# A two-layer chain of MLPs behind attention: the last 768 tokens of the first MLP as a 2x2 block product of seven multiplications

## The chip, the cores and the metric

The kernel runs on one core of one Trainium2 chip. The metric is the device time of one execution in microseconds, and the median of the runs is compared. A profile is one execution, recorded by the hardware. PE is the matrix engine, DVE the vector engine, ACT the scalar engine, POOL the GpSimd engine, SP the queue that issues nearly all transfers. Names such as `h<-xt,w` mean: this instruction writes tile `h` and reads tiles `xt` and `w`.

## The reference

Causal windowed attention over 4 sequences of 576 tokens (8 heads of 64, window 64) gives x of 2304 tokens by 512. Two MLPs follow; nothing is masked or routed:

```python
x = attention(q, k, v)                      # 2304 x 512
h = x @ moe_w_in                            # 512 -> 2048
x = softplus(h) @ moe_w_out                 # 2048 -> 512
gate = sigmoid(x @ moe2_w_gate)             # 512 -> 1536
out = (gate * (x @ moe2_w_val)) @ moe2_w_out    # 1536 -> 512
```

The weights come in a wide format as pairs of 32-bit words. The kernel makes of each value a part "hi" and a rest "lo", and each product is three matmuls: hi*hi, hi*lo, lo*hi (`mm3`).

## The kernel before

**Attention.** 36 groups of 64 query tokens (all heads at once): scores on PE, maximum and exponential on DVE and ACT, the sum's reciprocal, the scaling on POOL, a transposition, and the product with the values on PE (`att_scores` to `att_values`). The first 8 groups run ahead of the first MLP. The transposition is on PE for the groups of the first two token blocks (`att_transpose`); for the others DVE transposes 32x32 pieces and two transfers through DRAM finish it (`att_blocks`, `att_send`, `att_fetch`). `att_hi` and `att_lo` write the result as hi and lo into the block's tile `xt`.

**First MLP.** The tokens stand in five blocks, `BLOCKS1 = [512, 384, 384, 512, 512]`. For each block and each of 16 slices f of 128 hidden features, `m1_proj` makes h (4 chunks of the 512 inputs, 12 matmuls, each as wide as the block), ACT takes softplus (`m1_act`) and splits off hi (`g_hi`), DVE makes lo (`g_lo`), and `m1_out` adds the slice's share to four accumulators (12 matmuls). PE runs `m1_out` two projections behind `m1_proj`; h has two PSUM banks, so the projection after next waits for `g_lo`. A finished block is copied out of PSUM and sent to DRAM (`m1_copy`, `m1_send`, tensor `x2d`).

**Weights of the first MLP** are split once, during the first block: `w_scale` on ACT, `w_shift`, `w_sign`, `w_low` on DVE, `w_hi` on ACT, `w_lo` on DVE, one pair of slices (w1 of f, w2 of f-2) for each projection.

**Second MLP.** It already uses the scheme of seven products: 768 tokens at a time (two halves of 384, `HALF`), the inputs' two halves, and gate and value as the two column blocks. For each of 12 slices, seven sums of weight blocks were made while the first MLP ran (`c_sums`, `c_sum4`, split in `c_hi`, `c_lo`, stored to DRAM with `c_send` as `wcd`) and come back as `wc` (`wc_load`, 1792 KB, two buffers). Seven sums of token blocks are made per 768 tokens (`x2_load`, `x2_sum`, `x2_hi`, `x2_lo`). PE makes seven products of 6 matmuls with 384 columns (`m2_prod`), DVE recombines them (`m2_after`, helper `tt`), and `m2_out` adds to six accumulators of 128 tokens each, with 18 matmuls of 512 columns.

**What sets the order.** The PE order is written out (`slots`). Everything else ahead of the second MLP is placed on its engine by a planner in the kernel (`lead_in`): it walks through the work with due times from `events`, costs from `traits` and a few weights in the constants, and emits one fixed order for each engine. Each engine then works in that order, so an instruction that waits holds back all behind it on its engine. SP issues transfers in its own fixed order.

## Time and profile before

| what | us |
|---|---|
| median of three runs | 895.02 (894.74 to 895.33) |
| the profiled execution | 895.09 |
| its span, first to last instruction | 893.3 |
| PE busy in the span | 885.0 |
| DVE, ACT, POOL busy | 523.8, 400.0, 153.8 |
| granted TensorE clock | 1.00 of full speed nearly throughout (mean 0.999) |

Three stretches follow each other: the lead-in to 31 us, in which attention for the first 512 tokens runs and weights arrive; the first MLP with the rest of attention, from 31 us to 471 us; the second MLP, from 471 us to the end. A matmul's record is longer than its share of the stream, since one starts before the last has ended; what one costs is read from start to start.

### The profile page before, as it was taken

To read this page: it belongs to the slowest core of one execution; us is meant where nothing else is said; L and a number is where in the kernel's file an instruction comes from. 1 tells how busy PE (TensorE), PEld (TensorE's weight loads), DVE (VectorE), ACT (ScalarE), POOL (GpSimd) and SP (SyncE) were. 2 spreads that over 40 slices of the span, in tenths; PEclk is the share of its full clock that TensorE was granted. 3 is DMA by queue.
4 is the path that set the end of the run, shared out by engine and by line. 5 is a ranking of instruction groups with operands and counts; after the bars stand their busy time and mean duration, and the time that the engine had idled before them with its cause. 6 is when DMAs were issued, how large, how long until landed. Compare 5 with 4: busy or idle time off the path is not lost.

```text
span 893.3 us, 13510 instructions
## 1 busy us (share of the span) xinstructions
PE 885.0 (99%) x5035; PEld 797.6 (89%) x5035; DVE 523.8 (59%) x921; ACT 400.0 (45%) x892; POOL 153.8 (17%) x157
## 2 busy tenths in 40 slices
PE   9999999999999999999999999999999999999997
PEld 7788789999999888888889999999999999999996
DVE  4898876556555756455515667668445447444444
ACT  6867857546764755345323333334222125222222
POOL 4001102102110220002001333331111112111110
PEclk9999999999999999999999999999999999999999
DMA  9946346766885764683307565545454445544441
GB/s 349 397 151 210 134 163 210 246 199 226 270 268 205 243 234 165 209 287 130 130 1 256 220 254 203 208 174 216 179 209 159 159 164 209 183 165 165 165 165 72
DMA packets 56210, 177.58 MB, mean 199 GB/s; under 512 B 6096, under 2 KB 21456, under 8 KB 51536
## 3 DMA queue, kind: packets, MB, share of 16 engines
q1 hardware_dynamic: 56000, 176.58, 56.0%
q8 instruction: 40, 0.66, 0.3%
q14 instruction: 26, 0.21, 0.1%
q10 hardware_dynamic: 144, 0.13, 0.0%
HBM read 139.72 MB, written 36.96 MB: 198 GB/s over the span
## 4 chain that ended last, share of the span: by engine, by line
PE 97%; DVE 1%; ACT 1%; POOL 0%; issue 0%; POOLq 0%
PE h L394 17%; PE h L396 17%; PE h L395 17%; PE acc L394 11%; PE acc L395 11%; PE acc L396 11%; PE at L289 3%; PE at L376 2%; PE at L396 2%; PE at L395 2%; PE at L394 2%; PE acc L289 1%; PE h L406 1%; PE acc L338 0%; POOL w L330 0%; PE at L338 0%
## 5 line engine op out<-in xcount | busy, mean ns | idle before, releaser
L512 DVE TENSOR_TENSOR w<-h,w 128x384 f32<-128x384 f32 x216 | 117.0, 556 | 159.7 <-PE h L396 157.0
L394 PE MATMUL h<-w,wc 128*128 128x384 f32 x504 | 169.0, 335 | 0.1
L396 PE MATMUL h<-w,wc 128*128 128x384 f32 x504 | 169.0, 335 | 0.0
L395 PE MATMUL h<-w,wc 128*128 128x384 f32 x504 | 168.8, 335 | 0.0
L524 POOL TENSOR_TENSOR g<-w,g 128x384 fp32r<-128x384 f32 x70 | 74.0, 1057 | 296.7 <-ACT g L517 252.1
L394 PE MATMUL acc<-g,w 128*128 128x512 f32 (+1 forms) x320 | 119.5, 374 | 0.0
L394 PE MATMUL h<-xt,w 128*128 128x512 f32 (+1 forms) x320 | 119.4, 373 | 0.1
L396 PE MATMUL h<-xt,w 128*128 128x512 f32 (+1 forms) x320 | 117.9, 368 | 1.0 <-DVE w L187 1.0
L396 PE MATMUL acc<-g,w 128*128 128x512 f32 (+1 forms) x320 | 117.7, 368 | 0.0
L395 PE MATMUL acc<-g,w 128*128 128x512 f32 (+1 forms) x320 | 117.6, 368 | 0.0
L395 PE MATMUL h<-xt,w 128*128 128x512 f32 (+1 forms) x320 | 117.6, 368 | 0.0
L436 DVE TENSOR_TENSOR g<-h,g 128x512 fp32r<-128x512 f32 (+1 forms) x80 | 50.7, 634 | 84.1 <-ACT g L430 83.8
L394 PEld LDWEIGHTS h<-w,wc 128*128 128x128 f32 x504 | 94.6, 188 | 2.4 <-DVE w L512 0.4
L395 PEld LDWEIGHTS h<-w,wc 128*128 128x128 f32 x504 | 94.6, 188 | 2.0
L396 PEld LDWEIGHTS h<-w,wc 128*128 128x128 f32 x504 | 94.6, 188 | 0.0
L423 ACT ACTIVATE h<-h 128x512 f32<-128x512 f32 (+1 forms) x80 | 43.2, 540 | 108.7 <-PE h L396 108.3
L517 ACT CAST g<-w 128x384 fp32r<-128x384 f32 x72 | 36.9, 513 | 117.5 <-DVE w L512 117.5
L396 PEld LDWEIGHTS h<-xt,w 128*128 128x128 f32 x320 | 60.1, 188 | 9.2 <-DVE w L187 1.7
L394 PEld LDWEIGHTS h<-xt,w 128*128 128x128 f32 x320 | 60.1, 188 | 8.4 <-issue 0.6
L394 PEld LDWEIGHTS acc<-g,w 128*128 128x128 f32 x320 | 60.1, 188 | 8.0
L396 PEld LDWEIGHTS acc<-g,w 128*128 128x128 f32 x320 | 60.1, 188 | 7.6
L330 POOL TENSOR_TENSOR p<-p,st 128x512 f32<-128x512 f32 (+1 forms) x28 | 27.8, 996 | 226.2 <-DVE st L325 165.2
(129 smaller groups left out, 1440.9 us busy)
## 6 DMA issues: line engine op xcount, KB each, us to landing
wc<-wcd SPq DMA_DIRECT2D x36, 1792.0 KB, 7.3
qk<-in_qk SPq DMA_DIRECT2D x28, 512.0 KB, 5.1
wcd<-raw SPq DMA_DIRECT2D x24, 512.0 KB, 3.5
w<-in_w SPq DMA_DIRECT2D x16, 512.0 KB, 9.6
raw<-in_w SPq DMA_DIRECT2D x16, 512.0 KB, 4.6
v<-in_vt SPq DMA_DIRECT2D x25, 256.0 KB, 3.8
raw<-in_wg SPq DMA_DIRECT2D x12, 512.0 KB, 4.6
raw<-in_wv SPq DMA_DIRECT2D x12, 512.0 KB, 6.1
```

The lines of the kernel that those rows point to most:

```text
L289: nc.tensor.matmul(out=s[:, j, :w], lhsT=t[:, 0, j, :], rhs=t[:, 1, j, :w], start=g >= NG0, stop=g >= NG0 or j == NPAIR - 1)
L330: nc.gpsimd.tensor_tensor(out=p[:, :, :w], in0=p[:, :, :w], in1=st[:, 2, :].unsqueeze(2).to_broadcast([P, NPAIR, w]), op=ALU.mult)
L376: nc.tensor.matmul(out=o[h * Q:(h + 1) * Q, j, :], lhsT=v[:w, (2 * j + h) * Q:(2 * j + h + 1) * Q], rhs=pt[:w, h, j], start=True, stop=True)
L394: nc.tensor.matmul(out=o, lhsT=lh, rhs=rh, start=first, stop=False)
L395: nc.tensor.matmul(out=o, lhsT=lh, rhs=rl, start=False, stop=False)
L396: nc.tensor.matmul(out=o, lhsT=ll, rhs=rh, start=False, stop=last)
L406: nc.tensor.matmul(out=idle["out"], lhsT=t[:, 0, :P], rhs=t[:, 1], start=True, stop=True)
L423: nc.scalar.activation(out=t, in_=t, func=AF.Softplus)
L436: nc.vector.tensor_tensor(out=g[:, 1, :n], in0=t, in1=g[:, 0, :n].bitcast(F32), op=ALU.subtract)
L512: nc.vector.tensor_tensor(out=out, in0=a, in1=b, op=op)
L517: nc.scalar.copy(out=g[:, 0, :HALF], in_=t)
L524: eng.tensor_tensor(out=g[:, 1, :HALF], in0=t, in1=g[:, 0, :HALF].bitcast(F32), op=ALU.subtract)
```

## The change

The first MLP now runs 1536 tokens in three blocks of 512 as before, and the last 768 tokens by the scheme of seven products.

- `SPLIT = 4`: the second block's first four slices are done for each half of 256 tokens apart (`UNITS`), so that their first half needs four groups of attention instead of eight. These matmuls have 256 columns.
- The last 768 tokens' attention goes to DRAM as floats (`att_out`, `att_put`, tensor `x1d`) and comes back in quarters (`x2_load`).
- For each pair of w1 slices (8 "quads", `NQ1`), DVE adds hi and lo again (`c_join`), and the sums are made and stored like those of the second MLP. There are 20 sets `wcd` instead of 12, and 44 loads `wc` instead of 36.
- A quad: seven products (`s_prod`, 42 matmuls of 384 columns), a copy on ACT (`s_copy`), seven recombinations on DVE (`s_mix`), four softplus on ACT (`s_act`), four splits (`s_hi` on ACT, `s_lo` on DVE or POOL). `s_out` adds to six accumulators of 128 tokens with w2 as the moving operand: 12 outputs of 3 matmuls of 512 columns, in runs of three.
- The accumulators hold tokens in rows, while the second MLP reads features in rows. So each is transposed in 32x32 pieces by DVE on the way out (`s_drain`) and stored by four transfers (`s_send`) of 64 KB each, in pieces of 128 bytes.
- The planner has other numbers: attention, joins and sums are placed by times (`DENSE`, `NEXT`, `REST`, `COMBO1`, `COMBO2`), eight instead of six groups run in the first block's time, and a transfer behind the lead-in is allowed 0.8 instead of 1.5 us of margin (3.8 us for `x2_load`).

PE's matmuls by count, from the two programs: first MLP, 512 columns 1152 before and 1056 after; 384 columns 768 and 0; 256 columns 0 and 192; in the quads 336 of 384 and 288 of 512 columns. Transpositions of later groups on PE: 24 and 32. Scores, values, the lead-in's matmuls and the second MLP's are as many as before.

```diff
-BLOCKS1 = [512, 384, 384, 512, 512]
+BLOCKS1, NS1, SPLIT = [512, 512, 512], 1, 4
-SLACK, NEAR = 0.15, .3
+SLACK, NEAR = 0.15, 0.4
+DENSE, NEXT, REST = (6.9, 11.0, 9.6), (62.8, 97.8), (120.5, 273.9)
+COMBO1, COMBO2, WOF, WOG, XT = (144.2, 12.9), (237.5, 17.3), 9.0, 13.0, 33.91
+URGE, FAR_MARGIN, X_MARGIN, HURRY = 40, 0.8, 3.0, 1.5
...
+    def c_join(q, k):
...
+        nc.vector.tensor_tensor(out=c_bits(q)[:, k], in0=w[:, 0], in1=w[:, 1], op=ALU.add)
...
+        if b == 1 and SPLIT:
+            UNITS += [(b, 0, n // 2, 0, SPLIT), (b, n // 2, n, 0, SPLIT), (b, 0, n, SPLIT, NF1)]
...
+    def att_put(g):
+        t0 = g * Q - NT1
+        nc.sync.dma_start(out=x1d[:, :, t0:t0 + Q].rearrange("k p n -> p k n"), in_=x_t.pop(g))
...
+    def s_prod(s, f, k):
+        o = h_t[s, f, k] = psum(f"h{(7 * (s * NQ1 + f) + k) % 2}")[:, :HALF]
+        product(o, s, f, k)
+
+    def s_copy(s, f):
+        nc.scalar.copy(out=half(0, 0), in_=h_t.pop((s, f, 0)))
+
+    def s_mix(s, f, k):
+        m1, u2, lo, hi, sa = (half(0, i) for i in range(5))
+        o = h_t.pop((s, f, k))
+        if k == 1:
+            tt(u2, o, m1, ALU.add)
+        elif k == 2:
+            tt(sa, o, m1, ALU.add)
+        elif k == 3:
+            tt(lo, o, u2, ALU.add)
+        elif k == 4:
+            tt(hi, o, lo, ALU.add)
+            tt(u2, o, u2, ALU.add)
+        elif k == 5:
+            tt(lo, lo, o, ALU.subtract)
+        else:
+            tt(sa, o, u2, ALU.add)
...
+    def s_out(s, f, j, c):
+        g, w = g_t[s, f, j], w_t["w2", 2 * f + j % 3 % 2 + (j == 2)]
+        cols = slice(c * P % HALF, c * P % HALF + P)
+        mm3(token_acc(s, c), g[:, 0, cols], g[:, 1, cols], w[:, 0, :], w[:, 1, :], f == 0 and j < 2,
+            f == NQ1 - 1 and j > 1)
+
+    def s_drain(s, c):
+        x = x_t[s, "y", c] = main.tile([P, 512], F32, tag="stage", name="x2", bufs=STB)
+        nc.vector.transpose(out=x, in_=acc_t[s, c])
+
+    def s_send(s, c):
+        x, t0 = x_t.pop((s, "y", c)), NT1 + 2 * s * HALF + c * P
+        o = x2d[:, :, t0:t0 + P].rearrange("c (b x) n -> x (c b) n", x=32)
+        for a in range(4):
+            nc.sync.dma_start(out=o[:, :, 32 * a:32 * (a + 1)],
+                              in_=x[32 * a:32 * (a + 1)].rearrange("x (k t) -> x k t", t=32))
...
+        late_q = [(s_out, s, f, j, 3 * j + i) for j in range(2) for i in range(3)]
+        outs = tail
+        for entry in "M0 M1 o0 o1 o2 M2 M3 o3 o4 o5 M4 M5 a0 a1 a2 M6 a3 a4 a5".split():
...
+        tail = [(s_out, s, f, j, (0, 3)[j - 2] + i) for j in (2, 3) for i in range(3)]
...
-                done[key] = dma + 0.85 + MARGIN
+                done[key] = dma + 0.85 + (MARGIN if start < OPEN else FAR_MARGIN + X_MARGIN * (key[0] is x2_load))
```

Where the order moves, in three places. First DVE in the first block, about its projection of f = 11. Before, in the rows from the `g_lo` of f = 10 to that of f = 11 (`g<-h`, line 436; lines 187 and 164 are `w_lo` and `w_shift`, 303 and 306 the maximum of a group):

```order
L436 TENSOR_TENSOR g<-h_956,g 128x512
L187 TENSOR_TENSOR w_1007<-w_860,w_1007 128x512 x2
L187 TENSOR_TENSOR w_1032<-w_860,w_1032 128x512 x2
L164 TENSOR_SCALAR w_1050<-w_1050 128x1024
L303 SCALAR_TENSOR_TENSOR p<-at,mask 128x512
L306 TENSOR_REDUCE st<-p 128x4
L303 SCALAR_TENSOR_TENSOR p<-at,mask 128x512
L306 TENSOR_REDUCE st<-p 128x4
L436 TENSOR_TENSOR g<-h_1035,g 128x512
```

Now, the end of the same stretch (line 483 is `g_lo`, 196 `w_lo`, 177 and 182 `w_sign` and `w_low`, 359, 360 and 424 the end of two groups):

```order
L359 TENSOR_SCALAR st<-st 128x4
L360 RECIPROCAL st<-st 128x4
L424 TENSOR_TENSOR xt<-at,xt 128x4x64 x2
L177 SCALAR_TENSOR_TENSOR w_1081<-raw,w_1081 128x1024
L196 TENSOR_TENSOR w_1156<-w_1081,w_1156 128x512
L182 SCALAR_TENSOR_TENSOR w_1081<-raw,w_1081 128x1024
L483 TENSOR_TENSOR g<-h_1062,g 128x512
L402 COPY pt<-at 128x512
L483 TENSOR_TENSOR g<-h_1134,g 128x512
```

The `g_lo` of f = 11 has moved down past the second half of two groups and two more passes over weights, to two rows ahead of the next one.

Second, DVE beside the work on the last tokens of the first MLP. Before, in the last block (line 489 is `x2_lo`, 164 to 173 the three passes over a pair of weights of the second MLP):

```order
L436 TENSOR_TENSOR g<-h_4099,g 128x512
L489 TENSOR_TENSOR w_4150<-xn_t_3835,w_4150 128x384
L436 TENSOR_TENSOR g<-h_4137,g 128x512
L489 TENSOR_TENSOR w_4185<-xn_t_3836,w_4185 128x384
L164 TENSOR_SCALAR bits<-bits 128x1024
L168 SCALAR_TENSOR_TENSOR bits<-raw,bits 128x1024
L173 SCALAR_TENSOR_TENSOR bits<-raw,bits 128x1024
L436 TENSOR_TENSOR g<-h_4172,g 128x512
```

Now, from the start of the second quad (line 553 is `s_mix`, 595 `s_lo`, 173 to 182 the three passes, 215 to 217 `c_sums`, 247 `c_lo`):

```order
L553 TENSOR_TENSOR w_3650<-h_3807,w_3650 128x384
L173 TENSOR_SCALAR bits<-bits 128x1024
L177 SCALAR_TENSOR_TENSOR bits<-raw,bits 128x1024
L182 SCALAR_TENSOR_TENSOR bits<-raw,bits 128x1024
L553 TENSOR_TENSOR w_3650<-h_3840,w_3650 128x384
L553 TENSOR_TENSOR w_3650<-h_3848,w_3650 128x384
L247 TENSOR_TENSOR raw<-bits,raw 128x512
L595 TENSOR_TENSOR g_3866<-w_3650,g_3866 128x384
L215 TENSOR_TENSOR sums<-bits 128x256
L216 TENSOR_TENSOR sums<-sums,bits 128x256
L217 TENSOR_TENSOR bits<-bits 128x256
L553 TENSOR_TENSOR w_3650<-h_3874,w_3650 128x384 x2
```

Each recombination stands between passes that prepare weights of the second MLP, and the three passes stand ahead of the second and third.

Third, SP at the start of the second MLP. Before (line 461 is `m1_send`, 239 `wc_load`, 135 a load of `wo`):

```order
L239 DMA wc<-wcd_74 128x3584
L461 DMA x2d<-x_4528 128x512
L461 DMA x2d<-x_4531 128x512
L461 DMA x2d<-x_4534 128x512
L461 DMA x2d<-x_4537 128x512
L135 DMA raw<-in_wo 128x1024
L239 DMA wc<-wcd_75 128x3584
```

Now (line 616 is `s_send`, 257 `wc_load`, 144 a load of `wo`):

```order
L257 DMA wc<-wcd_83 128x3584
L616 DMA x2d<-x_4790 32x16x32 x4
L616 DMA x2d<-x_4799 32x16x32 x4
L616 DMA x2d<-x_4825 32x16x32 x4
L144 DMA raw<-in_wo 128x1024
L616 DMA x2d<-x_4857 32x16x32 x4
L616 DMA x2d<-x_4866 32x16x32 x4
L257 DMA wc<-wcd_84 128x3584
L616 DMA x2d<-x_4886 32x16x32 x4
```

Four stores of 256 KB have become 24 of 64 KB, 20 of which stand ahead of the third slice's `wc`.

## Rows read from the trace of the kernel before

**Rows 1.** The page: span, busy time by engine, chain that ended last by engine.

```profile
span 893.3 us, 13510 instructions
PE 885.0 (99%) x5035; PEld 797.6 (89%) x5035; DVE 523.8 (59%) x921; ACT 400.0 (45%) x892; POOL 153.8 (17%) x157
PE 97%; DVE 1%; ACT 1%; POOL 0%; issue 0%; POOLq 0%
```

**Rows 2.** Timeline of PE (start, length, line, names, shape), two projections, four slices apart.

```profile
427.14 0.39 PE L394 MATMUL h<-xt,w 128*128 128x512 f32 x1
...
448.90 0.39 PE L394 MATMUL h<-xt,w 128*128 128x512 f32 x1
```

**Rows 3.** Timeline of PE in the second MLP: outputs of 512 columns, then products.

```profile
600.24 0.39 PE L394 MATMUL acc<-w,g 128*128 128x512 f32 x1
...
601.63 0.33 PE L394 MATMUL h<-w,wc 128*128 128x384 f32 x1
...
602.67 0.33 PE L394 MATMUL h<-w,wc 128*128 128x384 f32 x1
```

**Rows 4.** Timeline of PE: the first product of two slices in succession, second MLP.

```profile
586.72 0.33 PE L394 MATMUL h<-w,wc 128*128 128x384 f32 x1
...
598.16 0.33 PE L394 MATMUL h<-w,wc 128*128 128x384 f32 x1
```

**Rows 5.** Timeline of PE: transpositions of two groups; scores of two groups.

```profile
76.74 1.03 PE L338 MATMUL at<-ident,p 128*128 128x128 f32 x8
...
122.10 1.95 PE L289 MATMUL at<-qk 128*128 128x128 f32 x16
```

**Rows 6.** Timeline of PE: the one idle time inside the first MLP, and its releaser.

```profile
94.46 0.50 PE L396 MATMUL h<-xt,w 128*128 128x512 f32 x1 [0.96 <-DVE w L187]
```

**Rows 7.** Busy time of the engines by stretch (us, and instructions).

```profile
core 0: us, PE busy (x) PEld busy (x) DVE busy (x) ACT busy (x) POOL busy (x), PEclk, DMA share, GB/s
34.00:134.00 100.00, 99.03 (x557) 81.85 (x556) 86.18 (x128) 73.71 (x144) 6.73 (x7) 1.00 0.53 188
134.00:300.00 166.00, 166.00 (x1152) 161.46 (x1151) 99.97 (x190) 100.80 (x248) 23.18 (x22) 1.00 0.69 227
300.00:470.00 170.00, 170.00 (x874) 140.82 (x873) 86.15 (x144) 79.97 (x169) 22.12 (x20) 1.00 0.53 177
```

**Rows 8.** Groups of DVE by line and shape: count, busy us, mean ns.

```profile
L512 DVE TENSOR_TENSOR w<-h,w 128x384 f32<-128x384 f32 x216 | 117.0, 556 | 159.7 <-PE h L396 157.0 <-issue 1.3 <-ACT w L533 1.2
L168 DVE SCALAR_TENSOR_TENSOR bits<-raw,bits 128x1024 uint32<-128x1024 uint32 x14 | 17.8, 1273 | 0.4
L306 DVE TENSOR_REDUCE st<-p 128x4 f32<-128x512 f32 x25 | 17.2, 686 | 0.9
L303 DVE SCALAR_TENSOR_TENSOR p<-at,mask 128x512 f32<-128x512 f32 x25 | 17.1, 684 | 16.0 <-PE at L289 15.8
L389 DVE TENSOR_TENSOR xt<-at,xt 128x256 fp32r<-128x256 f32 x36 | 14.4, 413 | 6.9 <-ACT xt L384 6.6
```

**Rows 9.** Waits: ACT's `w_scale` for the second MLP's weights (total, times, longest).

```profile
ACT bits L160 <- DMA raw<-in_wv: 11.9, 5, 3.8
```

**Rows 10.** Transfers: count, KB each, median us from issue to landing.

```profile
wc<-wcd SPq DMA_DIRECT2D x36, 1792.0 KB, 7.3
pt<-pd SPq DMA_DIRECT2D x84, 64.0 KB, 3.3
x2d<-x SPq DMA_DIRECT2D x12, 256.0 KB, 2.2
```

**Rows 11.** Timeline of PE: the first product of the second MLP.

```profile
470.67 0.33 PE L394 MATMUL h<-w,wc 128*128 128x384 f32 x1
```

More of the change, by code (lines that the diff above doesn't have):

```diff
@@ new lines, in c_hi, with c_lo, c_send @@
+    def c_hi(q, part):
+        t, o, _ = c_part(q, part)
+        nc.scalar.copy(out=o[:, :o.shape[-1] // 2], in_=t)
+    def c_lo(q, part, engine):
+        t, o, _ = c_part(q, part)
+        n = o.shape[-1] // 2
+        eng = nc.gpsimd if engine == "pool" else nc.vector
+        eng.tensor_tensor(out=o[:, n:], in0=t, in1=o[:, :n].bitcast(F32), op=ALU.subtract)
+    def c_send(q, part):
+        _, o, at0 = c_part(q, part)
+        nc.sync.dma_start(out=wcd[q][:, at0:at0 + o.shape[-1]], in_=o.bitcast(F32))
@@ new lines, in s_act, with s_hi, s_lo, token_acc @@
+    def s_act(s, f, j):
+        nc.scalar.activation(out=quad(j), in_=quad(j), func=AF.Softplus)
+    def s_hi(s, f, j):
+        g = g_t[s, f, j] = main.tile([P, 2, NMAX], F32R, tag="g", name="g1", bufs=GB)
+        nc.scalar.copy(out=g[:, 0, :HALF], in_=quad(j))
+    def s_lo(s, f, j, engine):
+        g = g_t[s, f, j]
+        eng = nc.gpsimd if engine == "pool" else nc.vector
+        eng.tensor_tensor(out=g[:, 1, :HALF], in0=quad(j), in1=g[:, 0, :HALF].bitcast(F32), op=ALU.subtract)
+    def token_acc(s, c):
+        if (s, c) not in acc_t:
+            acc_t[s, c] = psum(f"acc{c}") if c < KC else psum("at", 2)
+        return acc_t[s, c]
@@ new lines, in tile_kernel, with attention, put @@
+    timed = {}
+    def attention(g, t, near):
+        odd = g % 2
+        if near:
+            def put(off, order, fn, *args):
+                at(t + off, order, fn, *args)
+        else:
+            def put(off, order, fn, *args):
+                timed[fn, *args] = t + 2.9 * off + order / 400
+        far = grp_block[g][0] >= FAR
+        put(0, 20, att_scores, g)
+        put(1, -30, att_max, g)
+        put(2, -30, att_exp, g)
+        put(4 - near, -33, att_sum, g)
+        put(4 - near, -32, att_norm, g)
@@ new lines, in traits @@
+        if fn is s_hi:
+            f, j = rest
+            return "act", 0.42, [(s_act, a, f, j)], [("g", GB, (s_out, a, f, j, 2 if j % 2 == 0 else 5))]
+        if fn is s_lo:
+            return THIRDS, 0, [(s_hi, a, *rest)], []
+        if fn is s_out:
+            f, j, c = rest
+            deps = [(s_lo, a, f, j), (*slots[pos[fn, a, *rest] - 1], None)]
+            if f == 0 and j < 2 and a == 0:
+                deps += [(m1_copy, NB1 - 1, k) for k in range(KC)] + [(att_out, g) for g in grp_block if g * Q >= NT1]
+            elif f == 0 and j < 2:
+                deps += [(s_drain, a - 1, c)]
+            return "pe", 0.68, deps, []
@@ L925, in traits @@
         if fn is swap_pools:
-            return "none", 0, [(att_lo, g) for g in groups if g >= NG0], []
+            return "none", 0, [(att_values, g) for g in groups if g >= NG0], []
+        raise AssertionError(fn.__name__)
     def order_of(deps_of):
```

530 lines of the change are left out of this document (327 added, 203 removed).

## The prediction

> **What bounds the kernel now.** First the page: PE is busy for 885.0 of 893.3 us and carries 97% of the chain that ended last [rows 1]. So the time is PE's stream plus its idle time, 8 us in all, and other engines matter only where they make PE wait. Then the timeline, for what one matmul takes from start to start. Between the projections of 427.14 and 448.90 us lie four slices, 96 matmuls of 512 columns: 21.76 / 96 = 0.227 us [rows 2]. In the second MLP six of 384 columns take 602.67 - 601.63 = 1.04, or 0.173 each, and six outputs of 512 columns 601.63 - 600.24 = 1.39, or 0.231 each [rows 3]. Check: 42 x 0.1733 + 18 x 0.2307 = 11.43, and two slices stand 598.16 - 586.72 = 11.44 us apart [rows 4]. Then the stretches: in 34 to 134 us DVE is busy for 86 of 100 us, later for 51 to 60% [rows 7], and there lies the one idle time of PE inside the first MLP, 0.96 us, which DVE's `w_lo` ended [rows 6]. So the first block has two limits close to each other.
>
> **The change, part by part.** The sum is made against the profiled execution, 895.09 us, of which 893.3 is the span and 1.8 lies around it; the median, 895.02, is the same within 0.1.
>
> PE's matmuls. Removed: 768 of 384 columns, 768 x 0.1733 = 133.1, and 1152 - 1056 = 96 of 512 columns, 96 x 0.2267 = 21.8; together 154.9 us. Added in the quads: 336 products of 384 columns, 58.2, and 288 outputs with w2 as moving operand. These have the form of the second MLP's outputs, so I take 0.2307: 66.4. A quad is thus 15.6 us of PE. Added in the second block: 192 matmuls of 256 columns, a form that the trace lacks. From 512 to 384 columns the price falls by 0.053; once more gives 0.120. Bounds: half of the price for 512 columns, 0.113, and the whole price for 384, 0.173. A row near it speaks for the lower part: scores of 128 columns, each with weights of its own, go 16 to 1.95 us, at most 0.122 each [rows 5], so a change of weights doesn't hold PE for longer than that. 192 x 0.120 = 23.0 (21.8 to 33.3). Added together 147.6: **-7.3 us**. The seven products save an eighth of the projections of 768 tokens; fewer and longer instructions have little part in it.
>
> The Trainium skill bears on the 256 columns. "TensorE: Matmul & The Clock Gate", section "Back-to-back issue gap", gives columns / 2.4 + 2.5 ns, which is 0.109 us for 256 columns (an estimate from that page); by it the sum would be 2.1 us lower. The rows above disagree with that formula at both widths that they show, since it gives 0.216 for 512 columns where the trace has 0.227; I stay with the line through the rows.
>
> Attention. Scores and values are as many as before. Eight groups instead of six of the later ones are transposed on PE, and two groups cost 1.03 us [rows 5]: **+1.0**. Two groups fewer take the way through DRAM, which lies beside PE's work.
>
> Lead-in: the same instructions in a slightly different order, among them one PSUM copy moved from ACT to DVE. Its end hangs on the last group's `att_lo`, the first `w_lo` and a fixed number of warming matmuls behind the last values. 0, with 0.8 either way. The second MLP's matmuls are the same: 0 on PE.
>
> So far -6.3. What PE will wait for comes on top.
>
> The first block. Each group costs DVE 0.68 (mask and scale) + 0.69 (maximum) + 0.41 (`att_lo`) [rows 8] and two small ones, about 2.1 us, and 0.7 more where it copies the transposed piece; two more groups are 4.3 to 5.7 us in a stretch where DVE has 14 us free [rows 7], and PE's own work there grows by 4 us. The total fits; the order decides. I added the traced mean durations down DVE's rows from the first `g_lo` to that of f = 11: 64.8 us before, 72.8 now, while PE's rows between the projections grow from 61.1 to 62.8. That `g_lo` still comes before the projection that needs its bank, f = 13, 13 us of PE later. Tighter are the rests of the weights. By the same count the worst of before is w1 of f = 11, 4.1 us behind PE, and there the trace shows 0.96 us of waiting (DVE is faster than my count by some 2 us, and a matmul needs the rest third). Now the worst are w2 of f = 8, 4.5 behind, and w1 of f = 14, 4.4 behind. So PE waits about 1.4 us instead of 1.0 and perhaps a second time: +0.4 to +1, at worst all 5.7.
>
> The second block's start. Slices of 256 columns give ACT and DVE half as long (an output comes four times 1.44 = 5.8 us after its projection), while ACT's exponentials of two groups with two table loads stand in between, and the fourth copy of the first block's accumulators stands on ACT behind two splits of weights and two slices' softplus. I count that copy 0.7 us after PE wants the bank: +0.7, from 0 to 2.
>
> The quads. DVE: 7 recombinations at 0.556 and at most four `s_lo` at the same price, 6.1 us, and the three passes, sums and splits for the second MLP, 7 to 9 us: 13 to 15 of 15.6 us. The three passes stand ahead of the second and third recombination. From the quad's start: passes until 5.95; `s_mix` of products 2 and 3 until 7.1, wanted by products 4 and 5 at 8.3 and 9.3; `s_lo` of the first quarter until 8.5, wanted at 10.4; that of the second until 12.6, wanted at 13.5. Slack 0.9 to 1.9 us: 0 if nothing comes late. But the passes wait for ACT's `w_scale`, and that for a load: before, ACT waited five times for such loads, up to 3.8 us [rows 9]. Then DVE has less to do, and behind the passes there stood splits of an h two projections ahead. Now four of the eight or so that fall beside quads may be late, and the margin is 0.8 instead of 1.5. What exceeds the slack reaches PE: +0.7, from 0 to 5.
>
> The stores at the end. 24 stores of 64 KB instead of 4 of 256 KB, ahead of the third slice's `wc`; 1.5 MB in all. The nearest row is `pt<-pd`, also 64 KB, in pieces of 512 bytes: 3.3 us to landing [rows 10]. DVE's fourth transposition needs the first buffer back, 5.5 us after its first; four stores in flight together land in time. The third `wc` lands in 7.3 us [rows 10] and is wanted 11.4 us after its issue. 0, up to the rival below.
>
> Together -6.3 + 0.7 + 0.7 + 0.7 = -4.2, rounded with the lead-in: **890.8 us**.
>
> **The rivals.**
> *DVE becomes the bound.* All of the first block's extra DVE work reaches PE (+5.7 in place of +0.7): 890.8 + 5 = 895.8, no change. For it: 86% busy there, and PE has already waited for it. Against it: 14 us free, and the extra PE work in the same stretch.
> *Late loads in the quads.* Eight sets at up to 3.8 - 0.9 = 2.9 us of waiting would be 23 us; as many and as long as before (five, 11.9 together) leave 11.9 - 5 x 0.9 = 7.4, in place of 0.7: 897.5, slower. It decides from about 4 us on. For it: PE has only 0.9 us of cover there, and `wc` comes on top of the other transfers. Against it: the planner puts the loads 5.5 us ahead of `w_scale`, and the engines' transfer share in 300 to 470 us was 0.53.
> *Short stores are slow.* If the four stores of an accumulator went one after the other at 3.3 us, the buffer would be back after 13 us instead of 5.5, DVE would stand in the second MLP's first slices, and with three buffers for six accumulators the last would be 23 us late: up to 913. It decides once four stores take more than 9 us, since 3.5 us are covered. No row shows pieces of 128 bytes. The Trainium skill, "DMA: Bandwidth & Descriptors", section "Specifications", has a rule against them: under 512 bytes the engine reads, modifies and writes. No row here shows that; it is this rival's mechanism.
> *The full gain.* 256 columns at 0.113, no new waits, 0.8 from the lead-in: 895.1 - 6.3 - 1.3 - 0.8 = 886.7.
> *Half slices as dear as those of 384 columns.* +10.2: 901. The scores' 0.122 speak against it.
>
> **How the numbers follow.** A measurement of this kernel can tell about 0.2% (1.8 us) from no change: faster is below 893.2, slower above 896.8. The forecast, a gain with 1 to 4 us of new waits (888 to 893), 0.62; the full gain 0.14 (886 to 888); DVE as the bound, or waits that eat the gain, 0.13 (893.2 to 896.8); late loads 0.06, short stores 0.03, dear half slices 0.02 (all slower). Faster 0.76, same 0.13, slower 0.11. The range of 8 in 10 reaches from 886.3, the full gain, to 895: it leaves out all of the slower cases and a part of the no-change case.
>
> **What would show it.** PE busy near 880. The second MLP takes 893.3 - 470.67 = 422.6 us from its first product to the end [rows 11]; now 421.3, since its first slice takes in six outputs of the quads (4.2 us) instead of two slices' shares (5.4). Its first product comes at 467.8. Starts 0.120 apart for 256 columns, quads 15.6 apart. Idle PE released by `w_lo` between 75 and 125 us; by a copy of accumulators at the second block; none in the quads. The stores land in under 5 us, and no `wc` is waited for. Wrong would make it: idle PE released by DVE in every quad, quads of over 16 us, or a first product of the second MLP after 472.

## The result, and the profile of the changed kernel

The changed kernel takes **905.68 us** (903.9 to 908.59), the kernel before 895.0: 1.0122 times as long, 95% interval 1.0094 to 1.015. The forecast was 890.8, with a range up to 895.0. The execution that was profiled took 906.37 us. Its page, lines that answer to [rows 1]:

```profile
span 904.6 us, 13824 instructions
PE 884.4 (98%) x4995; PEld 782.5 (87%) x4995; DVE 589.9 (65%) x1051; ACT 420.1 (46%) x941; POOL 170.5 (19%) x172
PE 49%; DMA 1%; DVE 1%; SPq 0%; ACT 0%; issue 0%; DVEq 0%; ACTq 0%
```

PE is busy as long as before (885.0) where some 6 us less were forecast, and the span is 11.3 us longer, so PE stands idle for 20.2 us instead of 8.3. The chain names half as much of PE as before; for where the time went, the timeline says more. Product by product (PE; start, length, line, names, shape): two quads in succession, and the first product of the second MLP, to be set against [rows 11]:

```profile
415.43 0.33 PE L441 MATMUL h<-w,wc 128*128 128x384 f32 x1
...
431.13 0.33 PE L441 MATMUL h<-w,wc 128*128 128x384 f32 x1
...
481.82 0.33 PE L441 MATMUL h<-w,wc 128*128 128x384 f32 x1
```

An undisturbed quad takes 15.70 us, as forecast (15.6). The second MLP starts at 481.82 instead of 467.8. From there to the end it is 904.6 - 481.82 = 422.8, against 422.6 before. So nearly all of the loss lies ahead of the second MLP, and most of it is idle PE. Five of the stops (the bracket gives idle time and releaser):

```profile
266.65 0.50 PE L441 MATMUL acc<-g,w 128*128 128x512 f32 x1 [2.61 <-DVE x L498]
...
365.68 0.51 PE L441 MATMUL acc<-w,g 128*128 128x512 f32 x1 [1.41 <-ACT g L590]
...
437.27 0.44 PE L441 MATMUL h<-w,wc 128*128 128x384 f32 x1 [1.78 <-ACT w L566]
...
496.60 0.45 PE L441 MATMUL h<-w,wc 128*128 128x384 f32 x1 [1.00 <-ACT w L643]
...
506.78 0.41 PE L441 MATMUL h<-w,wc 128*128 128x384 f32 x1 [0.56 <-DMA wc<-wcd]
```

Ahead of the first four, an engine that works in order had stood still. On ACT and DVE (timeline, same columns), three rows before the stop at 266.65, then one each before those at 365.68, 437.27 and 496.60:

```profile
258.97 0.62 ACT L241 CAST raw<-sums 128x512 fp32r<-128x512 f32 x1 [4.12 <-DMA wcd<-raw]
...
259.62 0.69 DVE L247 TENSOR_TENSOR raw<-sums,raw 128x512 fp32r<-128x512 f32 x1 [4.05 <-ACT raw L241]
...
265.90 0.69 DVE L498 COPY x<-acc 128x512 f32<-128x512 f32 x1 [0.26 <-DMA wcd<-sumr]
...
364.08 0.59 ACT L498 COPY x<-acc 128x512 f32<-128x512 f32 x1 [4.28 <-DMA x2d<-x]
...
433.13 0.62 ACT L241 CAST raw<-sums 128x512 fp32r<-128x512 f32 x1 [5.37 <-DMA wcd<-raw]
...
494.41 0.72 DVE L610 STREAM_TRANSPOSE x<-at 128x512 f32<-128x512 f32 x1 [1.02 <-DMA x2d<-x]
```

At 258.97 and 433.13 ACT is about to split part `x` of the sums for a slice of the *second* MLP (`c_hi`, line 241), into the half of a "raw" slot from which part `a` is still being stored. Behind it on ACT stand the copies and softplus that PE needs, and DVE waits for the split (259.62). The copies of accumulators (`m1_copy`, line 498) and the transposed outputs (`s_drain`, line 610) wait in the same way for a slot of the "stage" ring of three, which the fourth sums and the outputs for `x1d` now share with them. These buffers are new, and the list of the change above does not name them. In the kernel before, parts `x` and `s4` (the fourth sum) of the second MLP's sums had a "raw" slot of their own (`sumr`), and its table of waits has no row of ACT waiting for `wcd`. Now, in the table of waits (total us, times, longest) and on the page (median us from issue to landing):

```profile
ACT raw L241 <- DMA wcd<-raw: 28.9, 9, 5.4
...
wcd<-raw SPq DMA_DIRECT2D x52, 512.0 KB, 5.9
```

Before, the stores of `wcd<-raw` landed in a median 3.5 us, and those of part `x` out of `sumr` in 5.0. For the like on both sides, the 256 KB stores of accumulators to `x2d`: 2.2 us before [rows 10], 4.9 now.

In the stretch of the longest stop the DMA engines are full. Busy time by stretch (as [rows 7]; the last two columns are the busy share of the DMA engines and GB/s), 240 to 300 us, first of before, then of after:

```profile
240.00:300.00 60.00, 60.00 (x421) 57.40 (x421) 37.64 (x72) 37.03 (x96) 7.10 (x7) 1.00 0.64 215
```

```profile
240.00:300.00 60.00, 55.56 (x338) 45.96 (x337) 42.88 (x72) 38.19 (x88) 7.16 (x8) 0.97 0.99 343
```

ACT and DVE are busy 38 and 43 of 60 us there, the DMA engines 0.99 of the time. In all 209.04 MB are moved instead of 177.58.

For the comparison of kernels I add up what PE lost: over successive matmuls, the distance from start to start minus the price that the same form has in the kernel before (its median: 0.227 and 0.230 for 512 columns, 0.173 for 384; 0.120 for 256). At these prices the matmuls cost 844.8 us before and 838.1 now, 6.7 less. The loss on top, by stretch (a stop counts where it ends):

```
                      31-134 134-240 240-300 300-350 350-482 482-540   all    MB   median us
before                   3.9     2.2     1.8     1.5     0.6     0.5  12.3  177.6   895.0
after                    5.8     4.7     8.2     1.0     7.2     2.4  31.3  209.0   905.7
no_sends                 5.5     3.1     6.3     1.5     4.2     2.5  25.5  196.2   901.2
free_slots               5.4     4.2     8.3     1.3     6.1     2.8  30.3  209.0   905.8
sends_only               5.5     3.9     8.7     1.0     6.7     2.2  30.4  209.0   904.0
few_loads                5.6     4.0     7.2     1.0     3.4     2.2  25.4  198.0   902.0
free_stage               6.2     4.2     9.9     0.9     6.3     2.8  32.5  209.0   905.1
sums_home                5.9     5.1     7.0     9.8     7.5     2.9  40.2  209.0   914.2
home_late                5.2     4.9     6.0     1.7     7.0    11.5  38.1  209.0   913.1
margin                   5.3     4.5     2.8     7.7    10.7     6.8  39.9  209.0   914.5
no_sends2                6.0     7.0     3.9     1.0     1.6     2.3  23.9  188.9   898.3
no_sends_all             5.6     3.1     4.0     0.9     1.6     2.6  19.8  176.0   895.0
no_sends_free            6.1     3.2     2.3     0.7     1.6     0.6  16.7  176.0   892.1
wide_out                 5.5     4.0    10.7     1.0     6.3     0.7  30.5  209.0   902.7
two_queues               5.3     4.3     9.2     0.9     6.8     2.5  31.1  209.1   906.8
far4 (matmuls 846.8)     5.8     4.2     3.3     0.4     1.6     2.0  19.0  199.1   902.5
far3_two (841.6)         5.4     4.4     5.3     6.2     5.1     2.5  30.7  205.1   913.3
before, more stores      3.8     3.8     3.0     1.5     2.3     0.7  16.8  199.6   899.0
```

The losses are those of one profiled execution each ("all" counts what lies behind 540 us too, about 2), the last column is the median of all runs. Check: -6.7 in matmuls, +19.0 of loss and -0.4 in the lead-in are 11.9, and PE's last matmul starts at 900.21 instead of 888.29. Of the 19.0, some 11 are idle time, some 3.3 a lower clock behind two of the stops (last section), and the rest small amounts. The expectations below reckon the loss against each kernel's own medians, which gave 26.4 for after and 7.7 in its third stretch.

### The profile page after: what moved, and what is told of

The parts are those of the page before. It is cut to its first block, busy times and chain, and to the rows that moved or that the text cites. A ratio compares the mean times of both kernels' runs of the same rounds, so it can differ in the third digit from the quotient of the medians.

```text
span 904.6 us, 13824 instructions
## 1 busy us (share of the span) xinstructions
PE 884.4 (98%) x4995; PEld 782.5 (87%) x4995; DVE 589.9 (65%) x1051; ACT 420.1 (46%) x941; POOL 170.5 (19%) x172
## 2 busy tenths in 40 slices
DMA packets 79475, 209.04 MB, mean 231 GB/s; under 512 B 25520, under 2 KB 39856, under 8 KB 73776
## 4 chain that ended last, share of the span: by engine, by line
PE 49%; DMA 1%; DVE 1%; SPq 0%; ACT 0%; issue 0%; DVEq 0%; ACTq 0%
PE h L441 10%; PE h L443 10%; PE h L442 10%; PE acc L443 4%; PE acc L442 4%; PE acc L441 4%; PE at L441 2%; PE at L442 2%; PE at L443 2%; DMA wc<-wcd 1%; SPq L616 0%; DVE w L553 0%; DMA x2d<-x 0%; ACT bits L169 0%; DVE x L610 0%
## 5 line engine op out<-in xcount | busy, mean ns | idle before, releaser
L553 DVE TENSOR_TENSOR w<-h,w 128x384 f32<-128x384 f32 x264 | 142.6, 555 | 171.8 <-PE h L443 167.1
L441 PE MATMUL h<-w,wc 128*128 128x384 f32 x616 | 207.3, 336 | 3.4 <-ACT w L566 1.8
L443 PE MATMUL h<-w,wc 128*128 128x384 f32 x616 | 207.2, 336 | 0.0
L442 PE MATMUL h<-w,wc 128*128 128x384 f32 x616 | 206.8, 336 | 0.0
L441 PEld LDWEIGHTS h<-w,wc 128*128 128x128 f32 x616 | 115.8, 188 | 8.6 <-ACT w L566 2.2
L442 PEld LDWEIGHTS h<-w,wc 128*128 128x128 f32 x616 | 115.8, 188 | 3.5
L443 PEld LDWEIGHTS h<-w,wc 128*128 128x128 f32 x616 | 115.8, 188 | 0.0
L441 PE MATMUL acc<-w,g 128*128 128x512 f32 x208 | 81.2, 391 | 1.4 <-ACT g L590 1.4
L443 PE MATMUL acc<-w,g 128*128 128x512 f32 x208 | 82.6, 397 | 0.0
L441 PE MATMUL acc<-g,w 128*128 128x512 f32 (+1 forms) x208 | 80.0, 385 | 2.6 <-DVE x L498 2.6
L442 PE MATMUL acc<-w,g 128*128 128x512 f32 x208 | 82.2, 395 | 0.0
L441 PE MATMUL h<-xt,w 128*128 128x512 f32 (+1 forms) x208 | 79.9, 384 | 0.3 <-ACT w L188 0.2
L443 PE MATMUL acc<-g,w 128*128 128x512 f32 (+1 forms) x208 | 78.0, 375 | 0.7 <-DVE w L196 0.7
L443 PE MATMUL h<-xt,w 128*128 128x512 f32 (+1 forms) x208 | 77.8, 374 | 0.0
L442 PE MATMUL h<-xt,w 128*128 128x512 f32 (+1 forms) x208 | 77.7, 373 | 0.0
L442 PE MATMUL acc<-g,w 128*128 128x512 f32 (+1 forms) x208 | 77.6, 373 | 0.0
L660 ACT ACTIVATE w<-w 128x384 f32<-128x384 f32 x36 | 18.9, 525 | 97.6 <-DVE w L553 97.4
L553 DVE TENSOR_TENSOR w<-w 128x384 f32<-128x384 f32 x72 | 40.1, 557 | 25.1 <-ACT w L660 21.5
L441 PEld LDWEIGHTS acc<-g,w 128*128 128x128 f32 x208 | 39.2, 189 | 10.4 <-DVE x L498 3.0
```

The lines of the kernel that those rows point to most:

```text
L441: nc.tensor.matmul(out=o, lhsT=lh, rhs=rh, start=first, stop=False)
L442: nc.tensor.matmul(out=o, lhsT=lh, rhs=rl, start=False, stop=False)
L443: nc.tensor.matmul(out=o, lhsT=ll, rhs=rh, start=False, stop=last)
L553: nc.vector.tensor_tensor(out=out, in0=a, in1=b, op=op)
L660: nc.scalar.activation(out=sb, in_=u2, func=AF.Sigmoid)
```

## The experiments

**Whose fault are the stops: bytes, held slots, or the sums' computation?** Four kernels with the order of after kept.

No stores of the first MLP's sums:

```diff
     def c_send(q, part):
+        if 0 < q < NQ1:
+            return
...
-        nc.sync.dma_start(out=t.bitcast(F32), in_=wcd[f + NQ1 * (s >= NS1)])
+        nc.sync.dma_start(out=t.bitcast(F32), in_=wcd[f + NQ1 if s >= NS1 else 0])
```

> The changed kernel with the order of all work kept, but the sums of the first MLP's weights are stored for the first of the eight quads only (12.5 MB of stores fewer), and all eight quads load that one set, so the output is another. The sums themselves are still computed, and their buffers come free when they are computed. Theory A (PE waits because transfers land late, or because their buffers are held until they land): the three long stops, at 266.65, 365.68 and 437.27 us with the half clock behind the last, go; 906.4 falls by 6 to 9, to 897 to 900. Rival B (ScalarE and VectorE have too much to do with the sums): 904 or more.

901.19 us, ratio to before 1.0068 (1.0053 to 1.0083). The stop at 437 us and its half clock (last section) are gone, those at the third block's start and in the first quad are not: part of A, less than expected. ACT still waits 27.0 us for `wcd<-raw`.

Slots of "raw" not held by stores:

```diff
         _, o, at0 = c_part(q, part)
+        if q < NQ1:
+            o = w_t["w1", 2 * q].rearrange("p e n -> p (e n)")[:, :o.shape[-1]]
         nc.sync.dma_start(out=wcd[q][:, at0:at0 + o.shape[-1]], in_=o.bitcast(F32))
```

> The changed kernel with sums and transfers kept, but the transfers of the first MLP's sums take the same number of bytes out of the weights that lie ready, instead of out of the buffer that the sum was written to: no buffer of the two is held until a transfer lands (what is stored is not the sum, so the output is another). Theory A1 (the two buffers, held by stores that land late, stop ScalarE and behind it the MLP): as good as without the stores, 897 to 900. Rival A2 (the transfers are late for everybody, whoever holds a buffer): 904 or more, with the DMA engines as busy as now. Rival B (compute): 904 or more.

905.84 us, 1.0117 (1.0102 to 1.0132): no gain. But ACT's row in the table of waits is nearly as before the edit:

```profile
ACT raw L241 <- DMA wcd<-raw: 28.0, 9, 4.9
```

All stores named `wcd<-raw` are the second MLP's in this kernel, since the first MLP's come out of the weights. So the edit freed slots that hardly anyone waited for. A1 falls for the first MLP's sums alone. For the second MLP's, which make these waits, no kernel freed the slots with the bytes kept, and A1 stays untested.

Stores without the sums (`c_join`, `c_sums`, `c_sum4`, `c_hi`, `c_lo` return for q < NQ1; `c_send` as in the kernel before this one):

> The changed kernel without the joins, sums and splits of the first MLP's weights on VectorE, ScalarE and GpSimd; the same bytes are stored at the same places of the order, out of the weights that lie ready (the output is another). Theory A1 (buffers held): 895 to 900, since no buffer is held either. Rival A2 (late transfers): 903 or more. Rival B (compute): 893 to 897, better than the kernel with free buffers by 5 or more.

903.97 us, 1.0088 (1.0065 to 1.011), loss 30.4 for 31.3. With the added work of DVE and ACT on the first MLP's sums taken away, the stops stay. Rival B falls.

Fewer loads:

```diff
     def wc_load(s, f):
+        if s < NS1 and f > 1:
+            wc_t[s, f] = wc_t[s, f - 2]
+            return
```

> The changed kernel, where the quads from the third on use again the sums that the first two loaded: six loads of 1.79 MB (10.75 MB) fewer between 365 and 482 us; the output is another. Theory A1 and A2 alike: the DMA engines are less busy from 365 us on, the stores land sooner, and the stop at 437 us with its half clock goes, 3 to 4 us: 902 to 903.5, with the stops ahead of 365 us as they are. Rival B (compute): 905 or more, the stop at 437 us stays.

901.95 us, 1.0071 (1.0056 to 1.0086). This kernel changes neither a sum nor a store nor a buffer that a store holds, and the loss from 350 to 482 us falls from 7.2 to 3.4: the stop at 437 us is gone, stores land in a median 4.3 us instead of 5.9, and ACT waits 18.2 us for them instead of 28.9. So bytes that others move make the stores late (A2), and the held slot hands that on.

**The ring of three, and the order.** Two of the stops that were left name slots of "stage" (theory C). First with the order of after kept, then with the halves of the fourth sum in another place, then with the second MLP's sums later, then with another margin in the planner.

```diff
         _, o, at0 = c_part(q, part)
+        if part == "s4":
+            o = w_t["w2", 12].rearrange("p e n -> p (e n)")[:, :512]
```

(and `att_put` stores out of the same weights)

> The changed kernel in the same order, but the fourth sums and the attention outputs of the third part are stored out of weights that lie ready, with the same bytes, instead of out of their slots of the three-slot ring that they share with the copies of the accumulators; so a slot is held for the length of a copy and not until a store lands (the output is another). Theory C (the four accumulator copies at a block's end need slots that late stores of others hold): the stop of 2.1 to 3.6 us at the start of the third block goes below 1 us, that of 1.2 to 1.7 in the first quad shrinks by half at least; 2.5 to 4 us less than 906, 902 to 903.5. Rival A2 (the stores are late for everybody, and the copies then wait for the landing of their own): 905 or more, with the stops still there and the row of DVE's copy naming x2d instead of sumr.

905.14 us, 1.011 (1.009 to 1.013). The stop at the third block's start shrank, but a later one at 289 us grew from 1.83 to 3.62: it is an `att_values` that waits for `pt`, fetched from DRAM through the same full engines. C is true of that stop in part and is not where the time is lost.

```diff
-                send_t[q] = main.tile([P, 512], F32R, tag="stage", name="sumr", bufs=STB)
-            return c_bits(q)[:, 0, HC:], send_t[q], 6 * DM
+            return c_bits(q)[:, 0, HC:], sum_t[q].bitcast(F32R), 6 * DM
```

(with the planner's rings and dependencies to match)

> The changed kernel, where the halves of the fourth sum are written over the buffer of the first two sums, which is dead by then, instead of into a slot of the ring of three; the result is the reference's, the planner knows the new waits and orders anew. Theory C: the stops at the third block's start and in the first quad go as in the kernel with the free slots, 902 to 904. Rival A2: 905 or more.

914.21 us, 1.0207 (1.0192 to 1.0223): 8 us worse. The planner orders everything behind anew, and a new stop of 6.43 us behind a `g_lo` ends at 301 us. A miss; which row of the new order does it was not followed up.

```diff
-COMBO1, COMBO2, WOF, WOG, XT = (144.2, 12.9), (237.5, 17.3), 9.0, 13.0, 33.91
+COMBO1, COMBO2, WOF, WOG, XT = (144.2, 12.9), (254.0, 18.2), 9.0, 13.0, 33.91
```

(on top of the edit before)

> As the kernel before in this list, and the second MLP's sums begin 16.5 us later in the plan, 254.0 and then every 18.2 us instead of 237.5 and every 17.3, so that 1.3 sets of them (each 1 MB of loads and 1.79 MB of stores) move out of the stretch from 240 to 310 us, where the DMA engines are busy nine tenths. Theory A2 (crowded DMA): the excess of 7.7 us from 240 to 300 us falls by 2 to 4 more, 899 to 902. Rival C alone: as the kernel before in this list, within 1 us. If the quads have no room for it either: a stop of 2 us or more behind 400 us takes the gain back.

913.08 us, 1.0185 (1.0161 to 1.021). Against the kernel with only the edit before, the stretch from 240 to 300 us loses 6.0 instead of 7.0, the stop that ended at 301 us is gone, and 11.5 us are lost behind 482 us. The loss moved; it did not go.

```diff
-URGE, FAR_MARGIN, X_MARGIN, HURRY = 40, 0.8, 3.0, 1.5
+URGE, FAR_MARGIN, X_MARGIN, HURRY = 40, 3.0, 3.0, 1.5
```

> The changed kernel, whose planner counts a transfer of the first MLP as landed 3.0 us later than it thinks instead of 0.8, so it places what waits for transfers later in each engine's order; bytes and work are the same. Rival O (only the order is too tight; the engines have room): 898 to 902, the rows of ScalarE that wait for wcd sink from 28.9 us to under 10. Theories A2 and C: 903 or more, since the same bytes go through the same slots.

914.47 us, 1.0207 (1.019 to 1.0224), and it teaches most of the four. Its row for the third stretch:

```profile
240.00:300.00 60.00, 59.72 (x377) 49.08 (x377) 41.92 (x75) 37.72 (x91) 8.79 (x8) 1.00 0.98 323
```

The DMA engines are as full as in after, and PE hardly stops: what waits for transfers stands later in the order, and ACT's waits for `wcd` sink from 28.9 to 5.2 us, as rival O had it. So full DMA engines alone don't stop PE; the order has its part. But then the attention outputs come back from `x1d` too late, and the first quad pays (PE):

```profile
349.09 0.69 PE L441 MATMUL h<-w,wc 128*128 128x384 f32 x1 [6.09 <-ACT w L527]
```

Around this stop the granted clock is half, for 13.6 us (last section).

So an order can choose where the loss shows. None of the three other orders tried made it disappear; that no order could was not shown.

**Taking the bytes away.** All stores of sums but the first set of each MLP, and those of the second MLP alone (`if q not in (0, NQ1): return`, `if q > NQ1: return` in `c_send`; loads take the set that is there):

> The changed kernel in the same order with all sums computed, but only the first set of each MLP's is stored (7 sets of 1.54 to 1.79 MB and 11 of 1.79 MB fewer, over 30 MB in all), and every load takes the one that is there (the output is another). Theory A (the DMA engines are full from 134 to 310 us and from 375 to 430 us, and what waits for a landing comes late, whoever waits): the excess over back-to-back matmuls, 26.4 us after 31 us against 12.1 of the kernel before, falls to 12 to 15, and the time to 892 to 896. Rival B (the added sums on ScalarE and VectorE, and the order they stand in): 899 or more, with 5 us or more of excess left from 240 to 300 us.

894.98 us, 1.0 (0.9991 to 1.0009). The order and all the computation of after are there, 33 MB are not, and 10.7 us are back. With the bytes, the waits for the halves that they hold are gone too (ACT waits 2.1 us for `wcd`), so this pair does not part the two. The third stretch:

```profile
240.00:300.00 60.00, 57.99 (x359) 47.90 (x359) 46.54 (x80) 41.69 (x98) 7.92 (x9) 1.00 0.83 279
```

> The changed kernel in the same order with all sums computed, but of the second MLP's only the first set is stored (19.7 MB fewer between about 260 and 445 us; the output is another). Theory A: the excess from 240 to 300 us falls from 7.7 to 3 to 5, as these stores fill that stretch, and the stop at 437 us goes: 898 to 901. Rival B: 903 or more. If the full DMA engines from 240 to 300 us come from the attention and the first MLP's sums instead: excess there 6 or more, time 901 to 903 from the quads alone.

898.29 us, 1.0032 (1.0021 to 1.0043), with 3.9 us lost from 240 to 300 and 1.6 from 350 to 482: as theory A expected. Over after and the four kernels that differ from it by transfers left out, the time follows the bytes: 209.0, 198.0, 196.2, 188.9 and 176.0 MB, 905.7, 902.0, 901.2, 898.3 and 895.0 us.

The other way round, the kernel before with more stores:

```diff
+        o = w_t["w2", 12].rearrange("p e n -> p (e n)")[:, :n]
+        nc.sync.dma_start(out=more[f % 2][:, at0:at0 + n], in_=o.bitcast(F32))
```

> The kernel before with every store of the second MLP's sums made twice, the second time out of weights that lie ready into a place that nobody reads: 21 MB more stores and 48 more issues from about 150 to 450 us, nothing else. Theory A (bytes alone, in a stretch that is already full to seven tenths, cost time on PE): slower than before by 3 to 8 us, with waits for wcd, pt or x2d landings in front of PE's stops. Rival B (bytes are free until an engine has too much compute): within 1 us of 895.

899.04 us, 1.0042 (1.0026 to 1.0057): 22 MB that nobody reads cost 4.0 us. That is 4.5 us of loss for 22 MB where after has 19.0 for 31.5: with the order and the buffers of before, bytes cost far less. One of its stops is a copy of accumulators, as in after (PE, 1.39 us idle behind `ACT x L457`, its `m1_copy`).

**The short stores.**

```diff
-        o = x2d[:, :, t0:t0 + P].rearrange("c (b x) n -> x (c b) n", x=32)
-        for a in range(4):
-            nc.sync.dma_start(out=o[:, :, 32 * a:32 * (a + 1)],
-                              in_=x[32 * a:32 * (a + 1)].rearrange("x (k t) -> x k t", t=32))
+        nc.sync.dma_start(out=x2d[:, :, t0:t0 + P].rearrange("c p n -> p c n"),
+                          in_=x.rearrange("p (c n) -> p c n", c=KC))
```

> The changed kernel, where each of the six output tiles of the seven-multiplication block is stored by one transfer in rows of 512 bytes instead of four in rows of 128 (at other places, so the output is another). Rival S (short stores and their 24 issues delay the second MLP's start): the excess of 2.1 us from 482 to 540 us falls to 0.6, as it is before: 1 to 2 us less, 904 to 905.5. Theory A: within 1 us of 906, since the stops lie ahead of these stores.

902.66 us (899.54 to 904.98), 1.0081 (1.0058 to 1.0105). The loss from 482 to 540 us falls from 2.4 to 0.7, so rival S holds for 1.7 us; the third stretch of the profiled execution loses 10.7 instead of 8.2 with the same order and bytes up to there, so what the rest of the 3 us hangs on I don't know. SP's queue in after at that place:

```profile
487.97 4.92 SPq L616 DMA_DIRECT2D x2d<-x  x9
...
493.52 5.49 SPq L616 DMA_DIRECT2D x2d<-x  x8
499.11 0.46 SPq L257 DMA_DIRECT2D wc<-wcd  x1
```

Nine issues take 4.92 us there, and the load `wc` for the product at 506.78, which waits for it, stands behind seventeen of them. The larger stop there, 1.00 us at 496.60, does not hang on `wc`: DVE had stood for 1.02 us ahead of a transposition (494.41 above), until a store gave its slot back.

```diff
-            nc.sync.dma_start(out=o[:, :, 32 * a:32 * (a + 1)],
+            (nc.scalar if a % 2 else nc.sync).dma_start(out=o[:, :, 32 * a:32 * (a + 1)],
```

> The changed kernel, result and bytes as they are, with 12 of the 24 issues of the block's output stores on ScalarE's queue instead of SyncE's. If the issues delay the second MLP's start: the excess of 2.1 us from 482 to 540 us falls by 1 or more, 904 to 905. If it is the short rows on the DMA engines: 2 us stay, 905.5 to 906.5. If ScalarE's issues hold up its copies instead: 906 or more.

906.82 us, 1.0121 (1.0104 to 1.0138), 2.5 us lost from 482 to 540, no gain. The trace shows why: SP issues `wc` at 494.77 instead of 499.11, and no product waits for it. But ACT's work now stands behind ACT's own issues, and the stop at 496.60 has become one of 1.84 us at 497.56. On ACT, ahead of it:

```profile
494.74 0.53 ACT L660 ACTIVATE w<-w 128x384 f32<-128x384 f32 x1 [2.45 <-DMA x2d<-x]
```

So SP's issues did cost the 0.56 us of the `wc`, and ACT's took 0.84 in its place.

**Does the forecast's sum come out when its waits are gone?** The kernel without stores of sums, with the wide output stores, and with `m1_send` out of weights that lie ready:

> The kernel without the stores of the sums (all but the first set of each MLP), and besides that the accumulators are stored out of weights that lie ready, so that a slot of the ring of three is held only for the length of its copy, and the block's outputs are stored in rows of 512 bytes in 6 issues instead of 24 (both give another output). If the forecast's terms for the matmuls and the lead-in were right and only its waits were not: the stop at the third block's start falls from 2.2 to under 1 us, the excess behind 482 us from 2.3 to 0.6, and the time from 895.0 to 890.5 to 892.5, the forecast's 890.8. Rival (the matmuls or the first block cost more than forecast): 894 or more.

892.14 us, 0.9966 (0.9956 to 0.9977), against 890.8 in the forecast: within the 890.5 to 892.5 expected. The losses in the two stretches went from 4.0 to 2.3 and from 2.6 to 0.6 us in the table. So of the 19.0 us that after loses more than before, 11.5 (31.3 - 19.8) go with the stores of the sums, 3.1 (19.8 - 16.7) with the slots held by `m1_send` and the short stores, and 4.4 stay, 2.2 of them in the first block. How the 11.5 divide between bytes and held halves is open. The forecast had 2.1 for all waits: its 890.8 is met within 1.3 us, with matmuls 0.4 us cheaper than forecast and waits of twice the size.

**Real bytes off, with the result kept.** `FAR = 4`, `FAR_MARGIN, X_MARGIN = 1.5, 2.3`: no group goes through DRAM for its transposition.

> The changed kernel with the result as it is, where the probabilities of all 20 later groups are transposed on PE instead of by a round through DRAM (about 10 MB of transfers in 256 KB sends and four 64 KB fetches a group fewer, between 134 and 340 us; 80 transposes of 0.107 us more, 8.6 us of PE), and whose planner counts landings 0.7 us later. Theory A: DMA from 240 to 300 us falls from 0.99 of the time to under 0.9 and the excess there from 7.7 to 3 to 5, PE pays 8.6: 906 to 911 in all, and the excess over back-to-back matmuls falls by 3 or more. Rival O (it is the order alone): no less excess than now, 912 or more.

902.47 us, 1.0081 (1.0068 to 1.0094), better than expected: 10 MB fewer, 8.7 us more of matmuls (846.8), and yet 3.2 us faster than after.

```profile
240.00:300.00 60.00, 60.00 (x398) 49.12 (x395) 43.95 (x81) 43.66 (x108) 10.53 (x10) 1.00 0.85 290
```

The loss falls from 31.3 to 19.0 us, with PE busy throughout that stretch. The planner's margin differs too, so this pair doesn't part bytes from order; leaving out 11 and 13 MB with the order kept (`few_loads`, `no_sends`) took 5.9 and 5.8 us off the loss, not 12.3.

`FAR = 3`, and the issues on two queues as above:

> The changed kernel with the result as it is, where the third block's 8 groups are transposed on PE (4 MB of transfers fewer, 32 transposes, 3.4 us of PE more), and 12 of the 24 output issues on ScalarE's queue. Theory A: 1 to 3 us of the stops from 240 to 300 us go for 3.4 us of PE: 904 to 907. If the stops there hang on the stores of the sums alone: 907 or more.

913.28 us, 1.0199 (1.0181 to 1.0217), a miss: 4 MB fewer leave the DMA engines at 0.98 from 240 to 300 us, and the new order has a stop of 3.00 us at 310 and more in the quads. No kernel tried is faster than the one before with the result kept.

## Why the prediction was wrong, step by step

- **PE's matmuls, right.** Forecast -7.3 + 1.0 + 0 = -6.3; measured -6.7 and -0.4 in the lead-in. 256 columns start 0.120 apart, as the line through the rows gave, and not 0.109 by the formula in the Trainium skill's "TensorE: Matmul & The Clock Gate", section "Back-to-back issue gap". An undisturbed quad is 15.70 us. The term "dear half slices" is out.
- **The first block, right in kind, too small in size.** Forecast +0.7 (from 0.4 to 5.7), measured 5.8 - 3.9 = +1.9. `w_lo` was among the releasers (0.73 us at 94.20), as forecast; the larger stop, 0.94 us at 91.85, was scores that waited for ACT's copy of a transposed piece (`pt`, line 402), which the sum does not have. The rival "DVE becomes the bound" (+5.7) did not come.
- **The second block's start, wrong.** Forecast +0.7 for a copy of accumulators; PE has no stop of over 0.4 us between 95 and 209 us. A copy of accumulators held PE up for 2.61 us at the *third* block's start instead. That copy is on DVE, which had stood for 4.05 us behind ACT's held-up split and then 0.26 us for a slot of "stage": late stores, where the prediction had an order on ACT. From 134 to 240 us the loss is +2.5 all the same, 1.17 us of it a stop at 209.99 behind `att_lo`; the rest, in gaps of some 0.1 us, was not followed up.
- **The quads, the step that failed most.** Forecast +0.7 "if nothing comes late", and nothing in 0.9 to 1.9 us of slack; measured 7.2 - 0.6 = +6.6 from 350 to 482 us. Two stops make half of it, 1.41 and 1.78 us, and the lower clock behind the second some 1.7 more. Neither hangs on the `w_scale` that I had suspected: ACT stood in `m1_copy` and in `c_hi`, waiting for stores to land. The rival "late loads in the quads" had the place and nearly the price (+7.4), but named the loads and got 0.06.
- **What the sum has no term for: 240 to 300 us, +6.4.** The prediction says of bytes only that two groups fewer go through DRAM "beside PE's work" and that the DMA engines' share was 0.53 in 300 to 470. It never adds up the bytes. They were there to count: 8 more loads of 1792 KB and 8 more sets of sums of the same size, some 29 MB of the 31.5 that were added. The 166 us whose share stood at 0.69 [rows 7] got 304 GB/s instead of 227, 13 MB more, a share of 0.89 in the mean and 0.99 from 240 to 300. The row itself puts full engines at 227 / 0.69 = 329 GB/s (an estimate); after reaches 343. Nor has the sum a term for the buffers that the second MLP's sums lost: ACT's nine waits, 28.9 us, are all for them. Which of the two weighs more is open.
- **The stores at the end.** Forecast 0, measured +1.9 from 482 to 540. Landing took 2.5 us in the median, so the rival "short stores are slow" did not come at its size; its mechanism did in small, 1.02 us of DVE waiting for a slot. The Trainium skill's "DMA: Bandwidth & Descriptors", section "Specifications", has transfers under 512 bytes fall short of line rate, with a read-modify-write. The trace of after bears out the first: its packets of 128 bytes took a median 13 ns, those of 256 bytes 18, of 512 bytes 27 and of 4096 bytes 159, so a byte is dearer in a short packet. The four lie near one line, and no step at 512 bytes shows. What the forecast left out besides is SP's time for the issues ahead of `wc`: it has `wc` issued 11.4 us before it is wanted, and in after it is issued 7.1 us before.
- **The tests.** PE busy 884.4 for "near 880": wrong; the lower clock and the small gaps count as busy. The first product of the second MLP at 481.82, behind the 472 that I had named as proof of error. The stretch from there on 422.8 for 421.3. Idle PE in the quads where none was to be: wrong, though six of the eight quads take 15.7 to 16.0 us. Stores in under 5 us: right. No `wc` waited for: wrong, 0.56 us. (The range starts at 886.3 and calls it the full gain, whose own sum is 886.7; nothing hangs on it.)

In one line: -6.3 was right, and the +2.1 of waits were +19.0.

## What to carry to other kernels

Before an edit that adds stores and loads "beside" the bottleneck, add up its bytes stretch by stretch and set them against the share that the profile shows: at 0.69 busy in the mean, a third more bytes already filled 60 us of the stretch to 0.99. When the DMA engines are full, the cost shows on an engine that works in order and waits for a buffer to come free, so look at both: how late the stores land, and which buffers now wait for them that did not before. Before a slot is freed as a test, read from the table of waits whose store holds it; here the test freed others, and 28.0 of 28.9 us of waiting stayed. A planner that takes transfers for landed at a fixed delay makes no room for full engines, and the one larger delay that was tried with nothing else changed only moved the stop.

## What was not expected of the hardware

Two stops cost PE more than their length. Behind those of 2.61 us at 266.65 and of 1.78 us at 437.27 the granted clock fell to 0.50, the lower of its two levels (1.2 instead of 2.4 GHz), and PE was busy at it throughout (columns as [rows 7], the clock is the third from the end):

```profile
268.00:271.30 3.30, 3.30 (x27) 2.87 (x25) 3.21 (x7) 3.26 (x5) 0.30 (x1) 0.50 0.93 210
438.70:442.00 3.30, 3.30 (x11) 2.91 (x10) 3.23 (x7) 1.46 (x3) 0.00 (x0) 0.50 0.18 71
```

That is 6.6 us of work at half speed, some 3.3 us lost (an estimate: half of it). The stops of 1.83 us at 289.37 and of 1.41 us at 365.68 had no such stretch behind them. The kernel with the other margin paid most: around its stop of 6.09 us it was at half for 13.6 us, in which PE worked 8.3:

```profile
347.40:361.00 13.60, 8.31 (x19) 5.92 (x20) 8.49 (x16) 7.43 (x17) 6.90 (x6) 0.50 0.65 243
```

The runs of before lie within 0.6 us (894.74 to 895.33), those of after within 4.7. That is not shown to come from full DMA engines: those of `no_sends_free`, with 33 MB less, lie within 5.1.
